# Masking only the own chunk columns of a query tile: a 240-column mask matmul cut to 40 columns in a fused chunk-selection attention and gated MLP kernel

## The chip, the cores and the metric

The kernel runs on one core of a Trainium2 chip. The metric is the device time of one execution in microseconds (us). Before the change it was 208.66 us (median of 3 executions, 208.53 to 208.81). The profile's span is about 1.7 us shorter than that time.

Engines in the profile: PE is TensorE's matmuls, PEld its weight loads, DVE VectorE, ACT ScalarE, POOL GpSimd, SP SyncE.

## The reference, cut to what matters

```python
# B=4, H=8, S=768, D=64; chunk = 32, nc = 24 chunks, top_k = 6
k_min, k_max = k_chunks.min(axis=3), k_chunks.max(axis=3)
ub = sum(maximum(q * k_min, q * k_max), axis=-1)         # bound for each query and chunk
causal = pos[:, None] // chunk >= arange(nc)[None, :]
ub = where(causal, ub, -1e9)
top_chunks = argsort(ub)[..., -top_k:]                   # the six best chunks of each query
mask = sel & (pos[:, None] >= pos[None, :])              # selected chunk, and causal
attn = softmax(where(mask, scale * q @ k.T, -1e9));  x = attn @ v
# then, on x with the heads side by side: relu(x @ w_in), layer norm of one half,
# spatial mix, gate, @ w_out
```

## The kernel before: the parts that matter here

The 32 heads are taken in 16 pairs. A pair's queries are handled in six tiles of 128. The first tile has only four chunks, so no choice is needed. For the other five, `ub` holds 2 heads x 24 chunks = 48 columns each, 240 in all, in one PSUM tile.

```python
NCH, CPT, NQT, P = 24, 4, 6, 128;  W = 2 * NCH          # CPT: chunks of one query tile

def init_masks():                                        # on POOL, once, at the start
    nc.gpsimd.memset(later, 0.0)
    lv = later.rearrange("p (t h c) -> p t h c", h=2, c=NCH)
    nc.gpsimd.affine_select(out=lv, in_=lv, compare_op=Alu.is_ge, fill=NEG, base=CPT,
                            channel_multiplier=1, pattern=[[CPT, NQT - 1], [0, 2], [-1, NCH]])
    ...
def bounds(self):                                        # once per pair: 1 + 10 matmuls
    ub = self.ub = ps_tr.tile([P, 512], F32, tag="tr", name="ub")
    mm(ub[:, 0:(NQT - 1) * W], lhsT=sub_chunk, rhs=later, start=True, stop=False)
    for qi in range(1, NQT):
        for m in range(2):
            mm(ub[:, (qi - 1) * W:qi * W], lhsT=self.rq[:, m, qi * P:(qi + 1) * P],
               rhs=self.km[:, m].rearrange("p h c -> p (h c)"), start=False, ...)
def top(self, step):                                     # maxima read chunks up to the own tile only
    ... nc.vector.max(self.max8[:, qi - 1, hi, :], ub[:, c0:c0 + CPT * (qi + 1)])
def triangle(self, hi):                                  # causal diagonal blocks, from the second batch on
    if self.b == 0: return                               # (pairs 0 to 3 mask with a matmul instead)
    nc.gpsimd.affine_select(out=blk, in_=blk, compare_op=Alu.is_ge, fill=0.0, ...)   # on e
def values(self, hi, blocks, ...):                       # reads e, after triangle
    mm(self.av[:, qi, :], lhsT=self.e[hi][:, c:c + P], rhs=self.v[hi][:, t, 0:D + 1], ...)

v_ring = [ring.tile([P, 4, NQT, D + 2], F16, name=f"vt{i}") for i in range(3)]
def load_v(g):                                           # v of two pairs, issued by POOL
    t = v_ring[g % 3]
    nc.gpsimd.dma_start(out=t...[:, :, 0:D], in_=source(v, b, 2 * hp, 4))
# ... steps of all pairs and of the MLP are laid out in "beats"; apart from the first beats
# on PE, a list scheduler then decides each engine's order from its own model of durations
```

POOL does two kinds of work: it issues all loads that convert to 16 bit (k, q, v and weights), and from the fifth pair on it does one causal select ("triangle") for each head. The word "select" below means that instruction.

The softmax here doesn't subtract the row's maximum and nothing guards it: scores larger than these inputs give would overflow.

## Time and profile before

| | before |
|---|---|
| time, median (range) | 208.66 us (208.53 to 208.81) |
| span in the profile | 206.9 us |
| PE / ACT / DVE / POOL busy | 187.8 / 158.1 / 154.5 / 80.5 us |
| the 16 mask matmuls | 4.4 us busy, median 264 ns each |

This is the table of stretches of before: from and to (us), length, then each engine's busy time with its number of instructions, the mean granted clock of PE, the busy share of DMA, GB/s.

```profile
core 0: us, PE busy (x) PEld busy (x) DVE busy (x) ACT busy (x) POOL busy (x), PEclk, DMA share, GB/s
0.00:20.00 20.00, 9.39 (x91) 6.97 (x92) 12.20 (x44) 14.74 (x24) 18.41 (x26) 1.00 1.59 98
20.00:76.00 56.00, 51.85 (x727) 37.55 (x726) 51.03 (x163) 51.14 (x109) 38.81 (x49) 1.00 2.06 155
76.00:153.00 77.00, 76.93 (x804) 46.44 (x802) 65.87 (x200) 64.39 (x141) 19.84 (x21) 1.00 1.22 145
163.00:207.00 44.00, 40.01 (x221) 18.85 (x219) 18.87 (x35) 18.38 (x34) 1.36 (x2) 1.00 0.41 113
```

Read it by stretch. In the first 20 us PE is idle half the time: latency. From 20 to 76 us PE, ACT and DVE are each busy for 91 to 93% and none is full, so instructions wait for one another. From 76 to 153 us PE has no gap: there each nanosecond of PE issue counts.

The group view of before shows one mask matmul at 277 ns in the mean (busy us, mean ns, then idle time before it):

```profile
L219 PE MATMUL ub<-later,sub_chunk 128*128 128x240 f16 x16 | 4.4, 277 | 0.7 <-ACT a L257 0.7
L140 POOL MEMSET later<- 128x240 f16 x1 | 0.4, 357 | 0.0
L142 POOL TENSOR_SCALAR_AFFINE_SELECT later<-later 128x240 f16<-128x240 f16 x1 | 0.5, 481 | 0.0
```

PE's order of time of before (start us, duration us) shows what it costs in a fed pipeline:

```profile
84.47 0.26 PE L219 MATMUL ub<-later,sub_chunk 128*128 128x240 f16 x1
84.58 0.41 PE L222 MATMUL ub<-km,rq 128*128 128x48 f16 x10
84.83 0.38 PE L266 MATMUL sc<-a,kh 128*128 128x384 f16 x2
```

The next matmul starts 0.11 us after the mask matmul, and the ten 48-column matmuls take 0.25 us together. What the change can save is in the first number, not in the 264 ns.

### The profile page before, as it was taken

How to read it: one execution, taken by the hardware profiler on the slowest of the kernel's cores; microseconds unless marked ns; L12 is line 12 of the kernel's file. 1: busy time of each engine (PE TensorE's matmuls, PEld its weight loads, DVE VectorE, ACT ScalarE, POOL GpSimd, SP SyncE). 2: the span in 40 equal slices, each digit the busy share in tenths (PEclk: the TensorE clock that was granted, in tenths of full speed). 3: DMA queues.
4: the chain of work that ended last, by engine and by line, in shares of the span. 5: the costliest groups of instructions: out<-in, count | busy, mean ns of one | idle time of the engine just before them, and what ended most of it. 6: DMA issues, size and time to landing. Idle time of an engine off the chain costs nothing.

```text
span 206.9 us, 5068 instructions
## 1 busy us (share of the span) xinstructions
PE 187.8 (91%) x1922; PEld 115.1 (56%) x1922; DVE 154.5 (75%) x454; ACT 158.1 (76%) x326; POOL 80.5 (39%) x100
## 2 busy tenths in 40 slices
PE   0368999898899999999999999999999999999992
PEld 0266776775666665656655656565555454444440
DVE  6467979989799989899797999887647456365520
ACT  4797989899998889785989996669999830666042
POOL 7997659596992463236114111111111110000000
PEclk9999999999999999999999999999999999999999
DMA  5999999999999999979998926648782124540356
GB/s 38 92 118 154 140 178 158 173 177 167 177 162 162 97 119 128 135 130 147 149 278 153 180 62 57 127 88 158 181 166 65 38 29 92 187 152 3 72 128 256
DMA packets 114424, 27.27 MB, mean 132 GB/s; under 512 B 109536, under 2 KB 110816, under 8 KB 114400
## 3 DMA queue, kind: packets, MB, share of 16 engines
q0 software_dynamic: 76544, 12.20, 89.8%
q1 hardware_dynamic: 37856, 14.75, 36.4%
q8 instruction: 15, 0.25, 0.5%
q14 instruction: 9, 0.07, 0.1%
HBM read 24.38 MB, written 6.29 MB: 148 GB/s over the span
## 4 chain that ended last, share of the span: by engine, by line
PE 69%; ACT 17%; DVE 8%; issue 2%; DMA 2%; POOL 0%; DVEq 0%; ACTq 0%; POOLq 0%
PE mlp L388 40%; PE sc L266 12%; ACT e L271 10%; PE acc L289 7%; PE kTp L170 2%; ACT a L257 2%; DVE kmm L178 2%; PE ub L222 2%; DMA k<-in_k_dram 2%; PE trm L251 2%; ACT vraw L398 1%; PE tr L205 1%; DVE vn L412 1%; DVE kmm L182 1%; ACT u L420 1%
## 5 line engine op out<-in xcount | busy, mean ns | idle before, releaser
L271 ACT ACTIVATE e<-sc 128x512 f16<-128x512 f32 x192 | 96.9, 553 | 14.8 <-PE sc L266 13.4
L266 PE MATMUL sc<-a,kh 128*128 128x512 f16 (+3 forms) x256 | 65.5, 308 | 2.1 <-ACT e L271 1.5
L388 PE MATMUL mlp<-w_in_sb,xT 128*128 128x512 f16 x192 | 53.0, 379 | 0.1
L278 POOL TENSOR_SCALAR_AFFINE_SELECT e<-e 128x768 f16<-128x768 f16 x24 | 20.9, 869 | 66.3 <-ACT e L271 66.3
L289 PEld LDWEIGHTS <-e 128*128 128x128 f16 x672 | 31.4, 97 | 17.0 <-DVE x L297 3.8
L388 PE MATMUL mlp<-vn,wsT 128*128 128x512 f16 x144 | 37.3, 379 | 0.0
L289 PE MATMUL acc<-vt,e 128*128 128x65 f16 x672 | 35.3, 193 | 0.7 <-DVE x L297 0.4
L266 PEld LDWEIGHTS <-kh 128*128 128x128 f16 x256 | 22.7, 98 | 13.3 <-issue 0.8
L437 ACT COPY o<-mlp 128x512 f32<-128x512 f32 x24 | 14.1, 586 | 19.5 <-PE mlp L388 19.1
L400 DVE BATCH_NORM_STATS2 stats<-vraw 128x6 f32<-128x512 f32 x24 | 16.6, 693 | 12.9 <-ACT vraw L398 12.5
L388 PE MATMUL mlp<-w_out_sb,gT 128*128 128x512 f16 x96 | 25.1, 379 | 0.0
L388 PEld LDWEIGHTS <-xT 128*128 128x128 f16 x192 | 17.2, 97 | 12.6 <-issue 0.4
L427 DVE SCALAR_TENSOR_TENSOR g<-mlp,b_col,u 128x512 f16<-128x512 f32 x24 | 17.9, 748 | 7.3 <-PE mlp L388 6.2
L232 DVE MAX8 max<-ub 128x8 f32<-128x8 f32 (+4 forms) x160 | 15.6, 165 | 5.1 <-PE ub L222 4.9
L388 PEld LDWEIGHTS <-wsT 128*128 128x128 f16 x144 | 12.9, 98 | 10.4
L178 DVE TENSOR_REDUCE kmm<-kTp 128x24 f16<-128x768 f16 x16 | 15.2, 948 | 3.7 <-PE kTp L170 2.7
L297 DVE TENSOR_TENSOR x<-acc,rec 128x384 f16<-128x384 f32 x32 | 17.6, 551 | 0.4
L336 POOL DMA_DIRECT2D qs<-in_q_dram x14 | 14.6, 1049 | 5.9 <-PE sc L266 5.9
L194 DVE COPY kh<-kTp 64x768 f16<-64x768 f16 x30 | 16.5, 549 | 0.5
L398 ACT ACTIVATE vraw<-mlp 128x512 f32<-128x512 f32 x24 | 14.4, 601 | 3.0 <-PE mlp L388 3.0
L420 ACT ACTIVATE u<-mlp 128x512 f16<-128x512 f32 x24 | 14.3, 598 | 1.7 <-PE mlp L388 1.5
L327 POOL DMA_DIRECT2D k<-in_k_dram x14 | 14.4, 1045 | 2.5 <-PE kTp L170 1.8
(67 smaller groups left out, 230.2 us busy)
## 6 DMA issues: line engine op xcount, KB each, us to landing
out_dram<-o SPq DMA_DIRECT2D x24, 256.0 KB, 2.3
vt<-in_v_dram POOLq DMA_DIRECT2D x8, 384.0 KB, 8.8
k<-in_k_dram POOLq DMA_DIRECT2D x14, 192.0 KB, 8.1
qs<-in_q_dram POOLq DMA_DIRECT2D x14, 192.0 KB, 7.5
ws_raw<-in_moe_w_spatial_dram POOLq DMA_DIRECT2D x6, 192.0 KB, 6.9
w_in_sb<-in_moe_w_in_dram POOLq DMA_DIRECT2D x8, 128.0 KB, 6.9
w_out_sb<-in_moe_w_out_dram POOLq DMA_DIRECT2D x4, 128.0 KB, 7.9
k<-in_k_dram POOLq DMA_DIRECT2D x4, 96.0 KB, 3.4
```

What stands on the lines that cost most here:

```text
L178: nc.vector.tensor_reduce(self.kmm[:, 0, :], self.kT.rearrange("d (c ch) -> d c ch", ch=CHUNK), axis=AX.X, op=Alu.max)
L194: copy(self.kh[hi][d0:d1], self.kT[d0:d1])
L266: mm(sc[:, col:col + n], lhsT=self.kh[hi][:, t * P:(t + 1) * P], rhs=self.a[:, q0 // P:(q0 + n) // P, hi, :], start=True, stop=not diag)
L271: nc.scalar.activation(out=self.e[hi][:, g * 512:g * 512 + width], in_=sc[:, 0:width], func=Act.Exp, scale=scale)
L278: nc.gpsimd.affine_select(out=blk, in_=blk, compare_op=Alu.is_ge, fill=0.0, base=0, channel_multiplier=-1, pattern=[[0, NQT], [1, P]])
L289: mm(self.av[:, qi, :], lhsT=self.e[hi][:, c:c + P], rhs=self.v[hi][:, t, 0:D + 1], start=first and n == 0, stop=last and n == len(blocks) ...
L297: nc.vector.tensor_tensor(self.x16[:, :, hi, :], in0=self.av[:, :, 0:D], in1=rec.to_broadcast([P, NQT, D]), op=Alu.mult)
L388: mm(st[group][:, 0:cols], lhsT=lhsT, rhs=rhs, start=(j == 0), stop=(j == n - 1))
L398: nc.scalar.activation(st["vraw"][:, ti, :], h, func=Act.Relu)
L400: nc.vector.bn_stats(stats, st["vraw"][:, ti, :])
L420: nc.scalar.activation(st["u"][:, ti, :], h, func=Act.Relu)
L427: nc.vector.scalar_tensor_tensor(g, in0=vs, scalar=b_col[:, ti:ti + 1], in1=st["u"][:, ti, :], op0=Alu.add, op1=Alu.mult)
```

## The change

The intent: only the four chunks of a tile's own 128 queries need a mask. Earlier chunks are always allowed. Later ones are never read by the maxima, and the score blocks that they would select are never computed. So the mask matmul writes 40 columns (five tiles, two heads, four chunks) instead of 240, and the mask is filled for 40 columns.

```diff
-    later = cp.tile([P, (NQT - 1) * 2 * NCH], F16)
+    later = cp.tile([P, (NQT - 1) * 2 * CPT], F16)
@@ init_masks
-        lv = later.rearrange("p (t h c) -> p t h c", h=2, c=NCH)
-        nc.gpsimd.affine_select(out=lv, in_=lv, compare_op=Alu.is_ge, fill=NEG, base=CPT,
-                                channel_multiplier=1, pattern=[[CPT, NQT - 1], [0, 2], [-1, NCH]])
+        lv = later.rearrange("p (t h c) -> p t h c", h=2, c=CPT)
+        nc.gpsimd.affine_select(out=lv, in_=lv, compare_op=Alu.is_ge, fill=NEG, base=0,
+                                channel_multiplier=1, pattern=[[0, NQT - 1], [0, 2], [-1, CPT]])
@@ bounds
-            mm(ub[:, 0:(NQT - 1) * W], lhsT=sub_chunk, rhs=later, start=True, stop=False)
+            own = bass.AP(ub.tensor, ub.offset + CPT, [list(ub.ap[0]), [W + CPT, NQT - 1], [NCH, 2], [1, CPT]])
+            mm(own, lhsT=sub_chunk, rhs=later, start=True, stop=False, skip_group_check=True)
             ...the ten 48-column matmuls, now with skip_group_check=True
```

The start flag now falls on a matmul that writes only 40 of the 240 columns. What the runs show of this is the output: every kernel with the 40-column matmul gave the right result.

More of the change, by code (lines that the diff above doesn't have):

```diff
@@ L222, in bounds @@
                     mm(ub[:, (qi - 1) * W:qi * W], lhsT=self.rq[:, m, qi * P:(qi + 1) * P],
-                       rhs=self.km[:, m].rearrange("p h c -> p (h c)"), start=False, stop=(m == 1 and qi == NQT - 1))
+                       rhs=self.km[:, m].rearrange("p h c -> p (h c)"), start=False, stop=(m == 1 and qi == NQT - 1),
+                       skip_group_check=True)
         def top(self, step):
```

## The prediction

> What bounds the kernel. The profile's span is 206.9 us (208.66 timed), granted clock 1.00 throughout. The table of stretches shows three regimes. 0 to 20 us is latency: PE is busy 9.4 of 20 us, and the chain of waits runs from loads through transposes, reductions and copies. 20 to 76 us: PE is busy 51.9 of 56 us, ACT 51.1, DVE 51.0, and the chain's largest item is the Exp on ACT (28%): nobody is saturated. 76 to 152 us: PE is busy all the time and nearly the whole chain is PE. The tail from 163 us has MLP matmuls only; the change isn't in it.
>
> What changes. 16 matmuls (one per pair of heads) shrink from 240 to 40 columns. The ten 48-column matmuls, the maxima and the comparison stay. Chunks beyond a tile's own four go unmasked, harmlessly: the maxima never read them, and the blocks they'd select aren't computed.
>
> The cost of one. The group view says 277 ns mean, 4.4 us in all, but that is mostly latency, which pipelining overlaps. In the order of time the next matmul starts 0.10 to 0.11 us after a mask matmul wherever PE is fed; the ten 48-column matmuls take 0.25 us, 25 ns each. [...] So 40 columns cost about 25 ns: 77 ns saved each. The group's busy time should fall by 84 ns each (slope between 240 and 48 columns: 264 against 183 ns), from 4.4 to about 3 us, medians near 180 ns. I expect no penalty for an output in runs of four columns.
>
> On the critical path. All 16: 1.2 us. Seven start in the saturated stretch (84.5 to 144.8 us): 0.54 us come off fully. Of the seven from 22 to 75 us perhaps a third counts: 0.2 us. After the first, PE waits 0.49 us for a copy anyway. On POOL, filling the mask (357 ns memset, 481 ns select) shrinks to perhaps 0.3 us: the second q load and later loads are issued about 0.5 us earlier. The chain from 5.7 to 20 us doesn't pass through those loads: 0.1 us.
>
> What moves. The scheduler reorders: 240 lines of difference in PE's 3846 rows (line numbers disregarded), all between rows 498 and 1783, about 30 to 80 us; ACT and DVE swap Exp groups with copies of a and k operands there. Elsewhere PE's order is the same. The single PSUM buffer shared by transposes and bounds is what such swaps can delay. I can't sign this: 0 +- 1 us, as large as the direct gain.
>
> Predicted: 207.8 us, between 206.2 and 209.4 (8 in 10). Faster by over 2%: 0.03; within 2%: 0.94; slower: 0.03.
>
> What would show it. Right: mask matmuls at ~180 ns, next start 25 ns later; the stretch from the tenth mask matmul to the last (84.47 to 144.79 us, 60.3 us, same order in both) about 0.5 us shorter; its start within 1 us of before; the tail still 44 us. Wrong: next start still 50 ns or more later; a start of that stretch moved by over 1 us (then the reordering decides); a tail that changes.
>
> What could make it wrong: the small matmuls' weight loads were hidden behind the 240 columns and surface; an unlucky order between 30 and 80 us.

The 77 ns rest on the trace of before: in the saturated stretch the next start comes 101 or 102 ns after a 240-column mask matmul. The 25 ns for 40 columns are the author's estimate, the same as measured for one of the ten 48-column matmuls (0.25 us together). The sum is 0.54 us for seven matmuls of the saturated stretch, 0.2 us for those before it and 0.1 us at the start, so 0.84 us off 208.66: 207.8 us.

## More of the kernel before

POOL's order of time of before, around the first select (line 278):

```profile
50.84 2.04 POOL L327 DMA_DIRECT2D k<-in_k_dram  x2 [0.67 <-PE sc L266]
52.93 0.86 POOL L278 TENSOR_SCALAR_AFFINE_SELECT e<-e 128x768 f16<-128x768 f16 x1
53.74 1.43 POOL L343 DMA_DIRECT2D vt<-in_v_dram  x1
55.17 0.56 POOL L363 DMA_DIRECT2D w_out_sb<-in_moe_w_out_dram  x1
```

POOL issues two k loads, does the first select, then issues a v load.

## The result, and the profile after

The changed kernel took 211.97 us (median of 4 executions, 210.7 to 212.6), beside 208.74 us for before. The ratio is 1.0146, with a 95% interval of 1.0108 to 1.0185: slower by 1.5%, outside the predicted range. A ratio is the mean time of one kernel's runs over that of the other's of the same rounds, so not quite the ratio of the medians.

The group view of after shows that the change did what it should to its own instructions:

```profile
L220 PE MATMUL ub<-later,sub_chunk 128*128 128x40 f16 x16 | 3.0, 189 | 0.6 <-ACT a L259 0.5
L140 POOL MEMSET later<- 128x40 f16 x1 | 0.2, 178 | 0.0
L142 POOL TENSOR_SCALAR_AFFINE_SELECT later<-later 128x40 f16<-128x40 f16 x1 | 0.3, 332 | 0.0
```

PE's order of time of after, for the same (tenth) mask matmul, now 30 ns ahead of the next start:

```profile
88.77 0.18 PE L220 MATMUL ub<-later,sub_chunk 128*128 128x40 f16 x1
88.80 0.41 PE L223 MATMUL ub<-km,rq 128*128 128x48 f16 x10
89.05 0.32 PE L268 MATMUL sc<-a,kh 128*128 128x384 f16 x1
```

But it starts at 88.77 us instead of 84.47. The stretches of after, the later ones cut 4 us later so that they hold the same work:

```profile
core 0: us, PE busy (x) PEld busy (x) DVE busy (x) ACT busy (x) POOL busy (x), PEclk, DMA share, GB/s
0.00:20.00 20.00, 9.18 (x92) 6.89 (x93) 12.23 (x44) 14.74 (x24) 18.11 (x26) 1.00 1.75 98
20.00:80.00 60.00, 53.59 (x727) 38.07 (x726) 51.28 (x164) 51.53 (x110) 38.79 (x49) 0.97 1.89 145
80.00:157.00 77.00, 76.76 (x801) 45.84 (x800) 65.96 (x199) 64.15 (x141) 19.84 (x22) 1.00 1.12 145
167.00:211.00 44.00, 39.83 (x221) 18.76 (x218) 18.87 (x35) 18.40 (x34) 1.34 (x2) 1.00 0.39 113
```

The same 727 matmuls that took 56 us take 60, and the granted clock there is 0.97. The other stretches hold the same work in the same time. The starts of the 16 mask matmuls place the loss more exactly, since each pair has one (differences of starts, read from PE's order of time in both profiles):

| stretch, by mask matmuls | before | after | change |
|---|---|---|---|
| start of the span to the 6th | 47.15 | 46.85 | -0.30 |
| 6th to 7th | 8.85 | 12.46 | **+3.61** |
| 7th to 8th | 7.80 | 8.92 | **+1.12** |
| 8th to 10th | 20.67 | 20.54 | -0.13 |
| 10th to 16th | 60.32 | 60.07 | -0.25 |
| 16th to the end | 62.11 | 61.96 | -0.15 |
| sum | 206.9 | 210.8 | +3.9 |

So the loss lies between 46.9 and 68 us. PE's order of time of after, there:

```profile
53.42 0.62 PE L291 MATMUL acc<-vt,e 128*128 128x65 f16 x15
53.88 0.50 PE L170 MATMUL kTp<-identity,k 128*128 128x128 f16 x6
56.52 0.36 PE L291 MATMUL acc<-vt,e 128*128 128x65 f16 x6 [2.14 <-POOL e L280]
```

The brackets say that PE sat idle for 2.14 us until POOL had written `e`: the first select. In before, the same six matmuls start without a wait:

```profile
54.05 0.35 PE L289 MATMUL acc<-vt,e 128*128 128x65 f16 x6
```

POOL's order of time of after:

```profile
50.94 2.04 POOL L329 DMA_DIRECT2D k<-in_k_dram  x2 [0.95 <-PE sc L268]
54.13 1.42 POOL L345 DMA_DIRECT2D vt<-in_v_dram  x1 [1.15 <-ACT e L273]
55.60 0.86 POOL L280 TENSOR_SCALAR_AFFINE_SELECT e<-e 128x768 f16<-128x768 f16 x1
56.42 0.57 POOL L365 DMA_DIRECT2D w_out_sb<-in_moe_w_out_dram  x1
```

The v load now stands ahead of the select. The compiled programs confirm that this is their order, with what each instruction waits for:

```
before:  select e_980        waits for ACT (the Exp of e), POOL
         load  vt1           waits for DMA completion counter 6, PE (last reads of vt1)
after:   load  vt1           waits for DMA completion counter 6, PE (last reads of vt1)
         select e_980        waits for ACT (the Exp of e), POOL
```

The select waited behind the load: POOL stood from 52.98 to 54.13 us although the select's inputs were ready (the group of Exps that holds its last one ended at 51.98 us). What it waited for is in the chain of waits of after (start us, us, what). There POOLq is POOL's sequencer, and "issue" is time in which the engine waited for nothing that the profile shows:

```profile
44.87 8.36 DMA k<-in_k_dram
53.23 0.02 issue
53.26 0.02 POOLq L345
53.27 0.84 issue
54.11 0.02 POOLq L280
54.13 0.77 POOL vt L345
54.90 0.69 issue
55.60 0.87 POOL e L280
56.47 0.05 issue
56.52 0.36 PE acc L291 x6
```

Completion counter 6 was last used by a k load issued at 44.87 us. That load landed at 53.23; 0.90 us later, at 54.13, the v load's issue began; it kept POOL for 1.42 us (384 KB; a k load of 192 KB takes about 1.02 us, half of the 2.04 us of two above); only then came the select. Of the 0.90 us the chain shows 0.84 as "issue". "ACT e" in POOL's view is the last of several semaphores, and not the one that held: the counter is. (The other condition, PE's last reads of the old v, is a group of 21 matmuls that ended before 50.5 us.)

There is a second loss. The stretches of 2 us of after show the clock of PE after the wait:

```profile
54.00:56.00 2.00, 0.38 (x8) 0.20 (x4) 0.81 (x2) 0.77 (x2) 1.82 (x2) 1.00 1.70 184
56.00:58.00 2.00, 1.48 (x16) 0.94 (x17) 1.08 (x3) 1.03 (x3) 2.00 (x3) 0.86 2.06 167
58.00:60.00 2.00, 2.00 (x20) 1.14 (x19) 1.29 (x3) 1.81 (x5) 2.00 (x4) 0.50 2.45 156
60.00:62.00 2.00, 2.00 (x29) 1.46 (x26) 1.13 (x11) 1.08 (x3) 2.00 (x4) 0.78 2.67 163
```

The clock is halved for about 3.4 us (from the means 0.86, 0.50 and 0.78 of three stretches of 2 us: 0.56 + 2.00 + 0.88). This dip came after a wait of 2.14 us, and the one in after_again below after a wait of 2.28 us; in one profile each, waits of 2.00 us (new_order_wide_fill) and 1.56 us (new_mm_old_order_2) were followed by a clock of 1.00. What decides whether a dip follows is not shown. Judging by the mean clock, not every execution has it. Of the ten timed executions of the changed kernel, five have a mean clock of 0.991 or 0.992 and average 212.6 us; five have 0.996 to 1.0 and average 211.2 us.

### The profile page after: what moved, and what is told of

Read it like the earlier page. It is cut to its first block, busy times and chain, and to the rows that moved or that the text cites. A ratio compares the mean times of both kernels' runs of the same rounds, so it can differ in the third digit from the quotient of the medians.

```text
span 210.8 us, 5068 instructions
## 1 busy us (share of the span) xinstructions
PE 189.1 (90%) x1922; PEld 114.9 (55%) x1922; DVE 154.8 (73%) x454; ACT 158.3 (75%) x326; POOL 80.2 (38%) x100
## 4 chain that ended last, share of the span: by engine, by line
PE 66%; ACT 12%; DVE 10%; DMA 6%; issue 3%; POOL 2%; POOLq 0%; DVEq 0%; ACTq 0%
PE mlp L390 41%; PE sc L268 11%; PE acc L291 7%; ACT e L273 6%; DMA k<-in_k_dram 6%; DVE kmm L178 2%; PE kTp L170 2%; PE ub L223 2%; DVE kmm L182 2%; ACT u L422 1%; DVE vn L414 1%; ACT vraw L400 1%; ACT a L259 1%; PE tr L205 1%; POOL vt L345 1%
## 5 line engine op out<-in xcount | busy, mean ns | idle before, releaser
L390 PE MATMUL mlp<-w_in_sb,xT 128*128 128x512 f16 x192 | 53.8, 383 | 0.3
L291 PE MATMUL acc<-vt,e 128*128 128x65 f16 x672 | 36.2, 194 | 2.8 <-POOL e L280 2.1
```

What stands on the lines that cost most here:

```text
L390: mm(st[group][:, 0:cols], lhsT=lhsT, rhs=rhs, start=(j == 0), stop=(j == n - 1))
```

## The experiments

The first theory: the shorter matmul is harmless, and it is the order that the scheduler chose that costs, above all the one pair on POOL. Rivals: the matmul itself costs (its strided output, or weight loads that 240 columns had hidden); or the order costs, but through its other moves (333 of 3845 places on PE, 52 on DVE, 27 on ACT).

To separate order from content, most kernels below hold every engine to a given order. At the end of the kernel, each engine's instructions are chained by edges that fix the order and add no wait:

```python
known = {i.name: i for i in nc.cur_bb.bb.instructions}
for text in chains.values():            # one list of names per engine, in the wanted order
    names = [n for n in ("I-" + x for x in text.split()) if n in known]
    for first, then in zip(names, names[1:]):
        tc.add_manual_dep(known[then], first, mybir.DependencyInfo(
            mybir.DependencyClass.NoSync, mybir.DependencyReason.DATA), reason="fixed order")
```

The built programs were compared with the one whose order they copy: each engine's order is identical, and with the new matmul in the old order the semaphore waits are too, but for three of PE's 3867 instructions. "Old order" is that of before, "new order" that of after. Each kernel was timed in five rounds beside before. The three groups of four ran on three chips; before's median was 208.69, 208.58 and 208.78 us there. "6th to 7th" is the distance of those mask matmuls' starts in each run's own profile (before: 8.85).

| run | matmul, fill | order | median us | ratio, 95% interval | 6th to 7th |
|---|---|---|---|---|---|
| new_mm_old_order | 40, 40 | old | 208.46 | 0.9988, 0.9974 to 1.0003 | 9.27 |
| old_mm_new_order | 240, 240 | new | 210.40 | 1.0099, 1.0076 to 1.0121 | 10.49 |
| new_order_triangle_first | 40, 40 | new, POOL pair swapped back | 209.06 | 1.0017, 1.0003 to 1.0031 | 9.44 |
| old_order_load_first | 240, 240 | old, POOL pair swapped | 210.09 | 1.0060, 1.0047 to 1.0073 | 10.27 |
| after_again | 40, 40 | new | 211.90 | 1.0161, 1.0129 to 1.0193 | 12.29 |
| new_order_4_v_buffers | 40, 40 | new, four v buffers | 209.43 | 1.0037, 1.0025 to 1.0049 | 9.84 |
| new_order_old_pool | 40, 40 | new, POOL's all old | 208.74 | 1.0018, 1.0001 to 1.0035 | 9.44 |
| old_order_load_late | 40, 40 | old, v load after the second select | 208.84 | 1.0016, 0.9988 to 1.0044 | 8.78 |
| new_order_wide_fill | 40, 240 | new | 210.87 | 1.0107, 1.0078 to 1.0137 | 11.54 |
| old_order_wide_fill | 40, 240 | old | 208.67 | 0.9998, 0.9981 to 1.0014 | 8.85 |
| old_mm_small_fill | 240, 40 | old | 208.64 | 0.9990, 0.9976 to 1.0005 | 8.85 |
| new_mm_old_order_2 | 40, 40 | old | 208.49 | 0.9980, 0.9963 to 0.9997 | 10.50 |

### new_mm_old_order: the new matmul, the old order

```diff
 (the changed kernel)
+    chains = {... every engine's order of before ...}
```

> The 40-column matmul and the small mask, but every engine's instruction order is held to that of the kernel before (chains of order-only edges; apart from the 16 matmuls and the two mask fills the program is the same). Theory (the order costs, not the matmul): no 2 us wait of PE for the triangle select, the granted clock stays near 1.00, and the time is 207.7 to 208.4 us, ratio to before 0.995 to 0.999; the stretch from the tenth to the last mask matmul is 0.2 to 0.5 us shorter than before's 60.32. Rival (the strided 40-column output or surfacing weight loads cost time): 210.5 us or more, ratio 1.01 or above.

Measured: 208.46 us, ratio 0.9988. The slowdown is gone with the order; in this order the matmul costs nothing that can be seen. The rival that blames the matmul alone falls. The time is just above the 207.7 to 208.4 us that the theory expected (the ratio is inside its range), and the interval includes 1: the gain is smaller than predicted, too. The stretch from the 10th to the 16th mask matmul is 60.13 us (before 60.32).

### old_mm_new_order: the old matmul, the new order

```diff
 (the kernel before)
+    chains = {... every engine's order of after ...}
```

> The 240-column matmul as before, but every engine's order is held to that of the changed kernel. Theory (the order costs): slow like the changed kernel, 211 to 213 us, ratio 1.010 to 1.020, with a PE wait of about 2 us for the first triangle select near 54 to 57 us and, in some executions, a dip of the granted clock after it. Rival (the matmul costs): 208 to 209 us, ratio below 1.003.

Measured: 210.40 us, ratio 1.0099. The 240-column kernel becomes slow when it is given the new order. That ratio is just under the 1.010 to 1.020 that were expected, and the PE wait was 0.87 us, not 2. PE's order of time of this run:

```profile
55.17 0.36 PE L289 MATMUL acc<-vt,e 128*128 128x65 f16 x6 [0.87 <-POOL e L278]
```

The clock was 0.996 or higher in all six executions. So the new order alone makes the kernel slower, but not by all of the 1.5%.

### new_order_triangle_first: one pair swapped back

```diff
 (the changed kernel, held to its own order, but on POOL:)
-    ..., load vt1, select e_980, ...
+    ..., select e_980, load vt1, ...
```

> The changed kernel with its own order on every engine, except that one adjacent pair on POOL is swapped back: the first triangle select goes before the v load instead of after it. Theory (this one pair costs): the 2.1 us PE wait for the select and the clock dip go, time 207.5 to 209 us, ratio 0.994 to 1.002. Rival (the 333 moved places on PE, or the other moves on ACT and DVE, cost): 210.5 us or more, ratio 1.009 or above.

Measured: 209.06 us, ratio 1.0017. Swapping one adjacent pair of POOL instructions back takes away nearly all of the loss. POOL's order of time of this run, then PE's:

```profile
52.18 0.86 POOL L280 TENSOR_SCALAR_AFFINE_SELECT e<-e 128x768 f16<-128x768 f16 x1
53.35 1.43 POOL L345 DMA_DIRECT2D vt<-in_v_dram  x1 [0.30 <-PE tr L205]
54.14 0.35 PE L291 MATMUL acc<-vt,e 128*128 128x65 f16 x6
```

The v load still has its wait, but nothing that PE needs stands behind it: the six matmuls start at 54.14 us without a wait, and in the profiled execution the clock stays at 1.00. The mask matmuls 10 to 16 are 59.86 us apart.

A version with a single order edge (that v load behind the first select) and the scheduler otherwise free builds to this order on every engine but POOL, where one w_out load comes ahead of the select as well. It was built and compared, and not run, so its time is not known.

### old_order_load_first: the same pair swapped in the kernel before

```diff
 (the kernel before, held to its own order, but on POOL:)
-    ..., select e_980, load vt1, ...
+    ..., load vt1, select e_980, ...
```

> The kernel before, 240 columns and its own order, except that one adjacent pair on POOL is swapped: the v load goes before the first triangle select. Theory (this one pair costs): a PE wait of 1.5 to 2.5 us for the select appears near 54 to 57 us, time 210 to 213 us, ratio 1.008 to 1.02. Rival (the other moves cost): 208.4 to 209.2 us, ratio within 0.3% of 1.

Measured: 210.09 us, ratio 1.0060, below the expected 1.008 but clear of the rival's 1.003. The wait appears, smaller than in after. PE's order of time of this run:

```profile
53.91 0.50 PE L170 MATMUL kTp<-identity,k 128*128 128x128 f16 x6
55.66 0.36 PE L289 MATMUL acc<-vt,e 128*128 128x65 f16 x6 [1.26 <-POOL e L278]
```

Here the counter was ready earlier: the v load's issue began at 53.27 us, not 54.13. So in this run the swapped pair makes PE wait for 1.26 us; in after, where the k load landed later, it was 2.14 us.

### after_again: the changed kernel, more executions

No edit.

> The changed kernel unaltered, for more executions beside the others. Theory: 210.5 to 212.6 us, ratio 1.009 to 1.017, the same as the 240-column kernel in this order (1.0099), because both have one order. Rival (the 40-column matmul makes the new order worse): stays at 1.014 or above, clear of 1.0099.

Measured: 211.90 us, ratio 1.0161, its profile like the first one's: a wait of 2.28 us and the clock at 0.50 from 58 to 60 us. The theory that both matmuls give the same time in this order is not met: 1.0161 is clear of the 1.0099 of the 240-column kernel (which ran on another chip). It is the rival's number that came; new_order_wide_fill below tests that rival again. The trace shows the difference in two terms, the v load's issue (54.08 us against 52.78) and the clock dip. The first term follows the shared counter. The packed traces record each landing on it, and in every profile with the load ahead of the select and three v buffers, the v load's issue begins 0.89 or 0.90 us after the last of them: 53.23 and 54.13 us in after, 53.18 and 54.08 here, 52.38 and 53.27 in old_order_load_first, 51.89 and 52.78 in old_mm_new_order.

### new_order_4_v_buffers: one more v buffer

```diff
-    v_ring = [... for i in range(3)]        t = v_ring[g % 3]
+    v_ring = [... for i in range(4)]        t = v_ring[g % 4]
 (the changed kernel, held to its own order, load before select)
```

> The changed kernel with its own order on every engine (the v load still ahead of the first triangle select), but four v buffers in place of three, so that the load has no earlier readers of its buffer to wait for. If the v load that blocks POOL is held by PE's last reads of the old v, it is issued about 0.8 us earlier and the PE wait for the select shrinks from 2.1 us to about 1.2; ratio about 1.003 to 1.008. If it is held by the k load that must have landed before it (they share a DMA completion counter), nothing changes: 1.009 to 1.015. Neither removes the 1.4 us that issuing the load takes on POOL.

Measured: 209.43 us, ratio 1.0037. POOL's order of time of this run shows the load before the select and no wait at all:

```profile
52.27 1.42 POOL L345 DMA_DIRECT2D vt<-in_v_dram  x1
53.74 0.86 POOL L280 TENSOR_SCALAR_AFFINE_SELECT e<-e 128x768 f16<-128x768 f16 x1
```

The ratio is inside the range of the first expectation (1.003 to 1.008), but its mechanism was not met: POOL's wait vanished, and PE waits 0.30 us where about 1.2 were expected. The run does not separate the two conditions, since it moved both: an earlier v load no longer waits for its buffer, and the k load on counter 6 was issued at 44.02 us instead of 44.83. Its last landing, at 51.62 us, came before POOL had finished the two k loads ahead (52.17), so the counter can hardly have held the v load here. In after it is the trace that decides (the chain above). The run does show that the issue of 1.42 us alone, without the wait ahead of it, costs PE little.

### new_order_old_pool: all of POOL's order restored

```diff
 (the changed kernel, held to its own order on PE, ACT, DVE and SP)
+    on POOL: the order of before
```

> The changed kernel with its own order on PE, ACT, DVE and SP and the whole POOL order of before. Theory (POOL's order is all that costs): 0.997 to 1.0005, as the new matmul in the old order (0.9988). Rival (the moves on PE, ACT and DVE cost the 0.3% that the triangle swap left over): 1.001 to 1.003, as with only the triangle swapped back (1.0017).

Measured: 208.74 us, ratio 1.0018, the same as with the one pair swapped back (1.0017). No cost of POOL's other moves shows. The rival holds for the rest: the moves on PE, ACT and DVE cost about 0.3% beside the 0.9988 of the old order (taken on another chip; the two intervals just overlap). The profile places it between the 6th and the 7th mask matmul, 9.44 us against 8.85 in before, and between the 7th and the 8th, 8.40 against 7.80.

### old_order_load_late: an attempt to beat both

```diff
 (the new matmul in the old order, but on POOL:)
-    ..., select e_980, load vt1, load w_out, select e_1067, ...
+    ..., select e_980, load w_out, select e_1067, load vt1, ...
```

> A version that should beat both: the 40-column matmul in the order of before, with that v load moved behind the second triangle select too. In the run with the old order this load waited 1.2 us on POOL with the second select behind it. Theory: 0.3 to 0.7 us less than the old order alone, 207.7 to 208.2 us, ratio 0.995 to 0.998. Rival (that wait is off the critical path, or the later load delays the values): 0.9985 or above.

Measured: 208.84 us, ratio 1.0016 with a wide interval (208.14 to 210.52 us). The expected gain is not there; the rival stands.

### new_order_wide_fill, old_order_wide_fill, old_mm_small_fill, new_mm_old_order_2: does the shorter fill matter?

The shorter fill lets POOL issue the following loads 0.3 us earlier (the first v load at 9.43 us instead of 9.70). The question was whether that shift makes the later k load land late, and so sets after apart from the old matmul in the new order.

```diff
 (wide fill: the 40-column matmul, a mask filled six times over)
+    later: 240 columns;  pattern=[[0, (NQT - 1) * 6], [0, 2], [-1, CPT]]
+    mm(own, lhsT=sub_chunk, rhs=later[:, 0:(NQT - 1) * 2 * CPT], ...)
 (old_mm_small_fill: the 240-column matmul reads the 40 columns six times; wrong on purpose)
+    mm(ub[:, 0:(NQT - 1) * W], lhsT=sub_chunk, rhs=later.unsqueeze(1).to_broadcast([P, 6, 40]), ...)
```

> The changed kernel with its own order and the 40-column matmul, but the mask's fill on POOL kept at 240 columns (the mask six times over; the matmul reads the first 40 columns). Theory (the shorter fill at the start shifts all later loads, so that the k load that blocks the v load lands about 1 us later; that is what sets 1.0161 apart from the 1.0099 of the 240-column kernel in the same order): loads as in the old kernel, PE wait for the first select about 1 us in place of 2.3, ratio 1.006 to 1.011. Rival (the 40-column matmul itself makes the new order worse): 1.014 or above.

> The 40-column matmul, the order of before, and the 240-column fill: only the 16 matmuls differ from before. Theory: the whole direct gain shows, 0.6 to 1.2 us, 207.4 to 208.1 us, ratio 0.994 to 0.997. Rival (the gain of the matmuls is lost to waits in any case): 0.998 or above.

> The kernel before in its order, with the small mask fill: the 240-column matmul reads the 40 filled columns six times over, so its mask is wrong on purpose and the output may be wrong. Theory (the shorter fill costs by shifting the loads): slower than before by 0.2 to 0.7 us, ratio 1.001 to 1.0035. Rival (it saves, or does nothing): 1.0005 or below.

> A repeat of the new matmul and small fill in the old order, beside the wide fill. Theory: 0.997 to 1.0005 again (0.9988), 0.2 to 0.8 us slower than the wide fill in the same order. Rival (the fill doesn't matter): equal within 0.15%.

Measured: in the old order the fill has no effect that can be told from noise (0.9998 with the wide fill, 0.9980 with the small one, 0.9990 for the old matmul with the small fill, whose output was wrong as intended). All three theories about the old order failed. In the new order the wide fill gave 1.0107, as the theory expected, against 1.0161, and below the 1.014 of the rival that blames the matmul. But the two intervals overlap at 1.013, they come from different chips, and the profiled execution still shows a wait of 2.0 us. Its last landing on counter 6 is at 53.28 us, as late as in after (53.23), which speaks against the theory's mechanism; what it lacks is the clock dip. Whether the fill has any part in the late landing stays open.

The profile of new_mm_old_order_2 (at 209.75 us the slowest of its seven executions) shows that the old order can lose time at the select too:

```profile
PE acc L291 <- POOL e L280: 1.6, 1, 1.6
```

There a w_out load further ahead had waited 1.56 us on POOL for the landing of a v load, and everything behind it, the select included, came late. This is the 10.50 us in the table, the same kind of loss through another load.

The direct gain is seen best in the intervals of the saturated stretch. From the 10th to the 16th mask matmul it is 60.32 us in before, old_mm_new_order and old_order_load_first. It is 59.84 to 59.86 in six profiles with the new matmul: 0.47 us less, for six matmuls (60.32 less 59.85). In the other four profiles with it, it is 60.03 to 60.29. In new_mm_old_order, one of these four, one of those intervals is 0.27 us longer. PEld's waits of that run, in the window 103 to 115 us (waiter, what for, us in total, times, longest):

```profile
PEld L268 <- DMA a<-qs: 0.6, 1, 0.6
```

A transposing load of `a` came late there; in new_order_triangle_first that wait was 0.3 us. In that run it gave back a part of what the shorter matmuls had saved; in the other three of the four the same wait is 0.5 to 0.8 us.

## Why the prediction was wrong, point by point

- **The cost of one mask matmul: right.** Median 181 ns (about 180 predicted), busy 3.0 us (about 3), next start about 30 ns later by the rounded starts above, 25 to 27 ns in after's trace for the seven of the saturated stretch (25).
- **The saving in the saturated stretch: right.** 0.54 us for seven means 0.46 for the six intervals measured; 0.47 came off where no other wait interfered, 0.25 in the profile of after.
- **The tail and the harmlessness of the unmasked chunks: right.** 44 us, right results.
- **The saving from 22 to 75 us and at the start (0.2 + 0.1 us): not seen.** In the old order, with the 40-column matmul, the ratio is 0.9980 to 0.9998, or 0.0 to 0.4 us of 208.7 us; the 0.47 us of the saturated stretch alone would be more. The intervals of these runs reach from 0.9963 to 1.0014, so terms this small can't be told from noise.
- **The step that failed** is the term "What moves": "The single PSUM buffer shared by transposes and bounds is what such swaps can delay. I can't sign this: 0 +- 1 us". It was mis-sized and put in the wrong place. The term measured +1.0% with the old matmul (1.0099, about 2.1 us) and +1.5 to 1.6% with the new one (about 3.0 to 3.4 us, what the matmuls save already taken off). It wasn't the PSUM buffer but POOL's queue: a load with an unmet condition stood in front of the select that PE needed. The order of both programs was at hand when the prediction was made, and the swapped pair is in it. The prediction counted PE's moved rows, named ACT and DVE, and did not read POOL's queue for who would be stuck behind whom.
- The prediction's own test said that a start of the saturated stretch moved by over 1 us means that the reordering decides. It moved by 4.30 us.

What is shown: one pair on POOL accounts for most of the loss, from both sides (from 1.0161 to 1.0017 when it is swapped back, and from 1 to 1.0060 when it alone is swapped in the kernel before). The rest of the new order costs about 0.3%. The clock dip came after the two longest waits that were profiled; executions with it take about 1.4 us more than those without (212.6 and 211.2 us), of which a part may be longer waits. What stays open: why the last landing on the shared counter comes at 53.2 to 53.3 us in after, after_again and new_order_wide_fill, at 52.45 in new_order_triangle_first (whose order is that of after up to the swapped pair) and at 51.89 in old_mm_new_order, and so why the same order costs 1.6% with the new matmul and 1.0% without. With one or two profiles of each kernel, this may be a difference between executions.

What made the scheduler change its order can be told from builds alone, with the scheduler free. With the new matmul and the wide fill, ACT and DVE have after's order; with the old matmul and the small fill, they have before's. So for ACT and DVE it is the matmul, not the fill. It is not so for the pair that costs: in both of these builds the select stands ahead of the v load, as in before. That pair swaps only when the matmul and the fill are both changed. Neither build was timed with the scheduler free.

## What to carry to other kernels

When a scheduler orders the instructions, a change is the edit plus a new order, and the order can outweigh the edit: compare the queues, and look in each for an instruction with a wait that stands ahead of one that another engine needs. Here that was a load issued by POOL: while it waited, the select behind it stood too, its inputs ready, and PE sat idle for 2.14 us. To tell an edit from its order, hold the order fixed both ways (new content in the old order, old content in the new); once the harmful pair is known, an order edge can keep it from coming back (here this was run only with the whole order held).
